# One attention-and-MLP kernel on one core: a reordered start, dummy matmuls, and heads 0 and 1 taken in turn

## The chip, the cores and the metric

The kernel runs on one core of one Trainium2 chip. The metric is the device time of one execution in microseconds (us). Two kinds of number appear below. The *time* of an execution is the metric; the *span* is what the profile of one execution covers, from its first to its last recorded instruction, and is 1.7 to 2.1 us shorter. TensorE is called PE, its weight loads PEld, VectorE DVE, ScalarE ACT, GpSimd POOL, SyncE SP. The *granted clock* is the profile's record of the share of full speed at which PE was allowed to run. A *bank* is a tile of PSUM, the memory that matmuls write to: transposes, Q and the output projection take theirs in turn from a ring of three (`mi_tile`), so a new one waits until the engine that reads the old one is done (in e6 below, 0.46 us from one Q matmul to the next for this reason, against 0.21 in e8).

## The reference

One transformer block with adaptive layer norm, 2048 rows of width 448, 16 heads of 256, an MLP of width 1792. Cut to what matters:

```python
mod = silu(c) @ w_mod                      # six vectors of 448: sa, ca, ga, sb, cb, gb
h = layernorm(x) * (1 + ca) + sa
q = h @ wq                                 # per head: 2048 x 256
p = softmax(q @ k_cache.T / 16)            # per head: 2048 x 2048
x = x + ga * ((p @ v_cache) @ wo)          # summed over 16 heads
h = layernorm(x) * (1 + cb) + sb
x = x + gb * ((gelu(h @ w_gate) * (h @ w_up)) @ w_down)
```

## The kernel before

The rows are cut into four row blocks of 512. A *unit* is one head times one row block: sixteen steps `j`, each with two score matmuls (`st`), one exp on ACT (`E`), two output matmuls (`oT`) and one addition of `E` to the row sums on DVE (`esum`). All other work of the attention (norms, Q projections, loads) hangs at chosen steps as `fill(u, j, f)`: `f` is emitted after step `j` of unit `u`. Engines execute in the order of emission, so a fill that waits blocks its engine (a Q fill at 50 us left PE idle for 0.43 and 0.28 us, with score matmuls emitted behind it).

The **prelude** is all that comes before the first scores: load x and w_mod, layer norm of row block 0, modulation columns, transposes, Q of head 0.

```python
    c_row load on ACT;  load_x(nc.sync, 0);  load_wm(0, WA)
    wq[0] = load_wq(0)
    kTs[0] = load_k(0, parts=2)          # DMA transposes, two halves
    load_x(nc.sync, 2); load_wm(WA, 3 * D); wos[0] = load_wo(0); load_x(nc.sync, 3)
    wq[1] = load_wq(1)
    ...                                  # (cut) silu of c
    load_x(nc.scalar, 1)
    vs[0] = load_v(0, nc.scalar)
    ...
    ln = LN(("a", 0), x_bf[0], ca1p_c, sa_c, mi_tile)
    for t in range(4):
        if t == 1:
            silu_c()
            modc = mod_cols(0)           # 32 one-column matmuls on w_mod
        ln.stats(t)
        if t % 2 == 1:
            ln.rstd(t - 1, 2)            # POOL
    mod_cols_out(modc, sa_c, ca1p_c)     # DVE
    for t in range(4):
        ln.norm(t)                       # DVE
    ln.twin(nc.vector)                   # last 64 columns once more, for rows 64..127
    for pr in range(2):
        ln.transpose(pr)                 # PE, evicted with the modulation by DVE and ACT in turn
    q_proj(0, 0)
```

The order of units, and the fills that feed row blocks 1 to 3:

```python
    units = [(h, r) for h in range(H) for r in range(NC)]
    ...
    pn = dict(on_pool=True)              # norm on POOL
    add_ln(("a", 1), x_bf[1], ca1p_c, sa_c, at(0, 0, 1, 2, 3), at(0, 3, 3, 3, 3), at(0, 10, 11), **pn)
    fill(0, 13, lambda: q_proj(0, 1))    # row block 1: transposes on PE
    add_ln(("a", 2), x_bf[2], ca1p_c, sa_c, at(0, 6, 7, 8, 9), at(0, 9, 9, 9, 9),
           (0, 14), at(1, 8, 9, 10, 11), **pn)
    fill(1, 13, lambda: q_proj(0, 2))    # row blocks 2 and 3: turned by DMA
    ...                                  # (cut) row block 3 likewise in units 1 and 2
            if r % 2:
                fill(u, 15, lambda u=u, h=h, r=r: (emit_exp(16 * u + 17), q_pair(h + 1, r - 1)))
```

"Turned by DMA" means: the normed block `xn` is written to DRAM (`xscr`), read back by four DMA transposes (`hT<-xscr`), and modulated in place on DVE (`modulate`).

The softmax here doesn't subtract the row's maximum and nothing guards it: scores larger than these inputs give would overflow.

## Time and profile before

| | before |
|---|---|
| time, median of 4 runs | 1245.64 us |
| span of the profiled execution | 1245.2 us |
| first score matmuls that run without a stall | 16.31 us |
| stalls of PE from there to 85 us | 5.0 us in ten places |
| first gate matmul of the MLP | 1106.82 us |

From the page of the kernel before (busy time by engine, then busy tenths in 40 slices, then the chain of waits; lines in between are left out, here and in the fences below):

```profile
span 1245.2 us, 17254 instructions
PE 1229.6 (99%) x5900; PEld 550.7 (44%) x5900; DVE 797.2 (64%) x1682; ACT 715.9 (57%) x1217; POOL 77.5 (6%) x93
PE   7999999999999999999999999999999999999998
PE 93%; DVE 2%; SPq 1%; DMA 1%; issue 1%; POOL 0%; ACT 0%; DVEq 0%
```

PE is the engine to watch, but 99% does not mean that 1% is left. In this trace the record of a 512-column matmul is 379 ns long, while such matmuls start 215.6 ns apart: records overlap, and their sum says little about how much time is left. So I read PE by the distance between starts: anything over 0.2156 us per 512 columns, the distance kept through the middle of the attention, I count as a stall, even where no idle time is shown.

The timeline of PE in the prelude of the kernel before (start, length, engine, line, operation, names, shape, count, then idle time before it and what ended it):

```profile
6.78 0.24 PE L190 MATMUL modc<-scT,wm 128*128 128x1 bf16 x3 [4.42 <-DMA wm<-in_w_mod_dram]
7.48 0.93 PE L190 MATMUL modc<-scT,wm 128*128 128x1 bf16 x29 [0.45 <-DMA wm<-in_w_mod_dram]
9.41 2.49 PE L278 MATMUL tp<-id_bf,xn 128*128 128x128 bf16 x16 [1.00 <-DVE xn L247]
11.69 0.63 PE L304 MATMUL qps<-hT,wq_t 128*128 128x512 bf16 x1
12.49 3.15 PE L304 MATMUL qps<-hT,wq_t 128*128 128x512 bf16 x7 [0.17 <-ACT hT L291]
15.43 0.63 PE L345 MATMUL st<-qT,kT 128*128 128x512 bf16 x1
16.31 1.24 PE L345 MATMUL st<-qT,kT 128*128 128x512 bf16 x5 [0.25 <-ACT qT L311]
```

The Q matmuls of the prelude stand about 0.43 us apart, twice the 0.2156 us: half clock. From 16.31 us on, five score matmuls start 0.2156 us apart. The trace's clock record fits: it begins at 16.09 us, with full clock (for the time before it has no entry).

What PE waited for in the kernel before, 16 to 90 us (total us, times, longest):

```profile
PE oT L538 <- ACT E L495: 1.3, 3, 0.8
PE qps L304 <- DVE hT L266: 0.7, 2, 0.4
PE st L345 <- ACT qT L311: 0.6, 2, 0.4
PE st L345 <- DVE qT L309: 0.4, 1, 0.4
PE tp L278 <- POOL xn L242: 0.3, 1, 0.3
```

These are the idle times that the view shows, 3.3 us in nine places, of which one (0.25 us) is the start at 16.31 itself. By the distance between starts the other eight and two more cost 5.0 us. Each says that a row block was needed soon after it was ready: Q waits for the modulated block, scores wait for Q, outputs wait for an exp that stood behind an eviction on ACT.

### The profile page before, as it was taken

The numbers are of one execution on the slowest core, as the hardware profiler recorded it, in microseconds if no ns is written. First come the engines' busy times: TensorE is split into PE (matmuls) and PEld (weight loads), VectorE is DVE, ScalarE is ACT, GpSimd is POOL, SyncE is SP. The second block draws the span as 40 slices with busy tenths as digits, with TensorE's granted clock in tenths as the row PEclk, the third lists the DMA queues.
The fourth block names the chain that finished last, engine by engine and source line by source line (L and its number), as shares of the span: only waits on it lengthen the run. The fifth ranks groups of instructions, "written<-read, shape, count | busy, mean of one in ns | idle before, by whom it ended". The sixth has DMA issues, their size and how long they took to land.

```text
span 1245.2 us, 17254 instructions
## 1 busy us (share of the span) xinstructions
PE 1229.6 (99%) x5900; PEld 550.7 (44%) x5900; DVE 797.2 (64%) x1682; ACT 715.9 (57%) x1217; POOL 77.5 (6%) x93
## 2 busy tenths in 40 slices
PE   7999999999999999999999999999999999999998
PEld 3444444444444444444444444444444444444443
DVE  6766666666666666676666666666666666776543
ACT  4556666666666666666666666666666666652222
POOL 4300000000000010020202010000000000000000
PEclk9999999999999999999999999999999999999999
DMA  7354032232423041402222221404041220030110
GB/s 189 85 135 97 18 64 55 47 115 51 119 40 93 28 95 43 101 18 52 63 47 67 51 67 37 82 13 97 18 83 35 48 54 18 18 85 16 49 49 16
DMA packets 181866, 76.48 MB, mean 61 GB/s; under 512 B 150161, under 2 KB 172242, under 8 KB 181778
## 3 DMA queue, kind: packets, MB, share of 16 engines
q1 hardware_dynamic: 180720, 73.87, 25.0%
q10 hardware_dynamic: 1058, 1.51, 0.5%
q8 instruction: 46, 0.75, 0.3%
q14 instruction: 42, 0.34, 0.1%
HBM read 33.67 MB, written 13.37 MB: 38 GB/s over the span
## 4 chain that ended last, share of the span: by engine, by line
PE 93%; DVE 2%; SPq 1%; DMA 1%; issue 1%; POOL 0%; ACT 0%; DVEq 0%
PE oT L538 34%; PE st L345 34%; PE wps L354 7%; PE qps L332 6%; PE dps L592 3%; PE g_ps L579 3%; PE u_ps L579 3%; PE qps L326 1%; PE g_ps L572 1%; DVE esum L535 1%; SPq L120 1%; DMA esT<-scr 0%; DMA scr<-esum 0%; DMA wq_t<-in_A_wq_dram 0%; PE qps L304 0%
## 5 line engine op out<-in xcount | busy, mean ns | idle before, releaser
L495 ACT ACTIVATE E<-st 128x512 bf16<-128x512 f32 x1024 | 608.3, 598 | 311.7 <-PE st L345 307.7
L538 PE MATMUL oT<-E,v_h 128*128 128x512 bf16 x2048 | 609.0, 379 | 1.9 <-ACT E L495 1.7
L345 PE MATMUL st<-qT,kT 128*128 128x512 bf16 x2048 | 609.5, 379 | 1.1 <-ACT qT L311 0.6
L535 DVE TENSOR_TENSOR esum<-esum,E 128x512 bf16<-128x512 bf16 x896 | 397.0, 443 | 163.4 <-ACT E L495 136.3
L538 PEld LDWEIGHTS <-v_h 128*128 128x128 bf16 x2048 | 199.6, 98 | 246.0 <-DVE oTn L501 10.6
L345 PEld LDWEIGHTS <-kT 128*128 128x128 bf16 x2048 | 200.3, 98 | 229.1 <-issue 1.9
L359 DVE SCALAR_TENSOR_TENSOR x_acc<-wps,inv,x_acc 128x448 f32<-128x448 f32 x240 | 163.7, 682 | 145.0 <-PE wps L354 145.0
L354 PE MATMUL wps<-wo_t,oTn 128*128 128x448 bf16 x512 | 138.6, 352 | 0.2 <-DVE x_acc L359 0.2
L140 POOL TENSOR_TENSOR wo_t<-wo_t,ga_bf 128x448 bf16<-128x448 bf16 x32 | 34.8, 1107 | 912.8 <-DMA wo_t<-in_A_wo_dram 781.0
L584 ACT ACTIVATE gl<-g_ps 128x512 bf16<-128x512 f32 x56 | 33.5, 598 | 89.5 <-PE g_ps L579 89.4
L332 PE MATMUL qps<-hT,wq_t 128*128 128x512 bf16 x360 | 82.9, 380 | 0.0
L354 PEld LDWEIGHTS <-oTn 128*128 128x128 bf16 x512 | 50.1, 98 | 60.7 <-issue 0.5
L337 DVE CAST qT<-qps 128x512 bf16<-128x512 f32 x60 | 41.5, 691 | 35.9 <-PE qps L332 35.6
L502 ACT CAST oTn<-oT 128x512 bf16<-128x512 f32 x64 | 37.6, 587 | 45.0 <-PE oT L538 45.0
L339 ACT CAST qT<-qps 128x512 bf16<-128x512 f32 x60 | 35.2, 587 | 46.8 <-PE qps L332 46.8
L585 DVE TENSOR_TENSOR hhT<-gl,u_ps 128x512 bf16<-128x512 bf16 x56 | 38.4, 687 | 36.1 <-PE u_ps L579 36.1
L332 PEld LDWEIGHTS <-wq_t 128*128 128x128 bf16 x360 | 32.8, 98 | 48.1 <-issue 12.7
L579 PEld LDWEIGHTS <-wgu 128*128 128x128 bf16 x336 | 30.6, 98 | 44.8 <-issue 11.9
L514 DVE TENSOR_REDUCE inv<-esT 128x4 f32<-128x512 bf16 x64 | 43.5, 679 | 4.5 <-DMA esT<-scr 4.5
L579 PE MATMUL g_ps<-hT,wgu 128*128 128x512 bf16 x168 | 45.7, 381 | 0.0
L579 PE MATMUL u_ps<-hT,wgu 128*128 128x512 bf16 x168 | 45.4, 379 | 0.0
L501 DVE CAST oTn<-oT 128x512 bf16<-128x512 f32 x64 | 44.2, 690 | 0.9 <-PE oT L538 0.9
(71 smaller groups left out, 317.1 us busy)
## 6 DMA issues: line engine op xcount, KB each, us to landing
scr<-esum SPq DMA_DIRECT2D x64, 128.0 KB, 2.0
wo_t<-in_A_wo_dram SPq DMA_DIRECT2D x16, 224.0 KB, 6.3
wq_t<-in_A_wq_dram SPq DMA_DIRECT2D x16, 192.0 KB, 5.0
xscr<-xn SPq DMA_DIRECT2D x6, 512.0 KB, 2.9
out_dram<-ob SPq DMA_DIRECT2D x16, 112.0 KB, 1.7
wd<-in_B_w_down_dram SPq DMA_DIRECT2D x2, 784.0 KB, 4.8
x_all<-in_A_x_dram SPq DMA_DIRECT2D x3, 448.0 KB, 4.1
wgu<-in_B_w_gate_dram SPq DMA_DIRECT2D x1, 1344.0 KB
```

The lines of the kernel that those rows point to most:

```text
L332: nc.tensor.matmul(qps[:], lhsT=wq[h][:, ch, dc * P:(dc + 1) * P], rhs=hT[("a", r)][:, ch, :], start=False, stop=(ch == 2),)
L337: nc.vector.tensor_copy(out=qTs[(h, r)][:, dc, :], in_=qps[:])
L345: nc.tensor.matmul(st[:], lhsT=kTs[h][:, dc, j * P:(j + 1) * P], rhs=qTs[(h, r)][:, dc, :], start=(dc == 0), stop=(dc == 1),)
L354: nc.tensor.matmul(wps[:], lhsT=oTn[:, dc, t * P:(t + 1) * P], rhs=wos[h][:, dc, :], start=(dc == 0), stop=(dc == 1),)
L359: nc.vector.scalar_tensor_tensor(out=x_acc[r][:, t, :], in0=wps[:], scalar=inv[:, t:t + 1], in1=prev[:, t, :], op0=ALU.mult, op1=ALU.add,)
L495: nc.scalar.activation(out=E[:], in_=sts.pop(g)[:], func=ACTF.Exp, scale=inv_sqrt_dh)
L501: nc.vector.tensor_copy(out=oTn[:, 0, :], in_=oT[0][:])
L514: nc.vector.tensor_reduce(out=inv[:], in_=esT[:], axis=mybir.AxisListType.X, op=ALU.add)
L535: nc.vector.tensor_tensor(out=esum[:], in0=esum[:], in1=E[:], op=ALU.add)
L538: nc.tensor.matmul(oT[i][:], lhsT=vs[h][:, j, i * P:(i + 1) * P], rhs=E[:], start=(j == 0), stop=(j == NKS - 1),)
L579: nc.tensor.matmul(ps[fc, i][:], lhsT=wgu[:, 3 * i + ch, fc * P:(fc + 1) * P], rhs=hr[:, ch, :], start=False, stop=(ch == 2),)
L585: nc.vector.tensor_tensor(out=hhT[:, fc, :], in0=gl[:], in1=ps[fc, 1][:], op=ALU.mult)
```

## The change

Its intent is to start the attention earlier and to feed its first units without stalls. Its core, with cuts:

```diff
-    kTs[0] = load_k(0, parts=2)
-    load_x(nc.sync, 2) ... load_x(nc.sync, 3)
+    vs[0] = kv.tile([P, NKS, Dh], BF16, name="v_h")
+    kTs[0] = load_k(0, parts=2, between=lambda i: v_part(vs[0], 0, 8 * i, 8 * i + 8, nc.sync))
     wq[1] = load_wq(1)
+    kTs[1] = load_k(1)
+    vs[1] = load_v(1)
...
-            in_=x2d[r * 512:(r + 1) * 512, :].rearrange("(t p) d -> p t d", p=P)
+        v = x2d[r * 512:(r + 1) * 512, :].rearrange("(p t) d -> p t d", p=P)   # out likewise
...
+    def warm_pe(n):                      # dummy matmuls, result unused
+        for _ in range(n):
+            nc.tensor.matmul(wpt[:], lhsT=id_bf[:], rhs=wz[:], start=True, stop=True)
+    warm_pe(10)
     load_x(nc.scalar, 1)
-    vs[0] = load_v(0, nc.scalar)
...
-    mod_cols_out(modc, sa_c, ca1p_c)
     for t in range(4):
+        if t == 2:
+            mod_cols_out(modc, sa_c, ca1p_c)
         ln.norm(t)
-    ln.twin(nc.vector)
-    for pr in range(2):
-        ln.transpose(pr)
-    q_proj(0, 0)
+        nc.scalar.copy(...)              # the twin of tile t
+        ...                              # four transposes of tile t
+        if t % 2:
+            warm_pe(1)
+    for ch in (0, 2, 1, 3):
+        ln.put(ch, tps[ch // 2][:, ch % 2, :], ch // 2)   # chunks 0,1 on DVE, 2,3 on ACT
+    q_one(0, 0)                          # chunk 3 as two half-height matmuls side by side
-    units = [(h, r) for h in range(H) for r in range(NC)]
+    units = [(h, r) for r in range(NC) for h in range(2)]
+    units += [(h, r) for h in range(2, H) for r in range(NC)]
...
+    fill(0, 12, lambda: q_one(1, 0))
+    fill(0, 0, load_rest)                # rest of w_mod, wo of head 0, x block 2
...
+    add_ln(("a", 1), x_bf[1], ca1p_c, sa_c, at(0, 1, 2, 3, 4), at(0, 6, 7, 8, 9), (0, 9),
+           at(1, 1, 2, 3, 4))            # norm on DVE, turned by DMA
+    ...                                  # blocks 2 and 3 likewise, two units later each
+    for r in range(1, NC):
+        fill(2 * r - 1, 11, lambda r=r: q_two(((0, r), (1, r))))
...
+            if (u, j) in fills:
+                emit_exp(g + 2)          # exp ahead of every fill
```

From head 2 on the units run as before.

More of the change, by code (lines that the diff above doesn't have):

```diff
@@ L102, in load_wq @@
         wq_t = wts.tile([P, DCH, Dh], BF16, name="wq_t")
-        if h == 0:
-            nc.gpsimd.memset(wq_t[DL:P, 3, :], 0.0)
         nc.sync.dma_start(
@@ L108, in load_wq @@
         )
-        for i in range(1 if h == 0 else 2):
+        for i in range(2):
             nc.sync.dma_start(
@@ L113, in load_wq, with load_k @@
         return wq_t
-    def load_k(h, parts=1):
+    def load_k(h, parts=1, between=None):
         kT = kv.tile([P, 2, SK], BF16, name="kT")
@@ L123, in load_k, with v_part, load_v @@
                 )
-        return kT
-    def load_v(h, eng=nc.sync):
+            if between is not None:
+                between(i)
+        return kT
+    def v_part(v_h, h, a, b, eng):
+        eng.dma_start(
+            out=v_h[:, a:b, :],
+            in_=A_v_cache[0, h, a * P:b * P, :].rearrange("(s p) d -> p s d", p=P),
+        )
+    def load_v(h):
         v_h = kv.tile([P, NKS, Dh], BF16, name="v_h")
-        eng.dma_start(out=v_h[:], in_=A_v_cache[0, h].rearrange("(s p) d -> p s d", p=P))
+        v_part(v_h, h, 0, NKS, nc.sync)
         return v_h
@@ L140, in scale_wo, with load_x @@
             nc.gpsimd.tensor_tensor(out=wo_t[:, cc, :], in0=wo_t[:, cc, :], in1=ga_bf[:], op=ALU.mult)
-    def load_x(eng, r):
-        eng.dma_start(
-            out=x_bf[r], in_=x2d[r * 512:(r + 1) * 512, :].rearrange("(t p) d -> p t d", p=P)
-        )
+    def load_x(eng, r, t0=0, n=4):
+        v = x2d[r * 512:(r + 1) * 512, :].rearrange("(p t) d -> p t d", p=P)
+        eng.dma_start(out=x_bf[r][:, t0:t0 + n, :], in_=v[:, t0:t0 + n, :])
     def load_wm(a, b):
@@ L157 @@
     wq[0] = load_wq(0)
-    kTs[0] = load_k(0, parts=2)
-    load_x(nc.sync, 2)
-    load_wm(WA, 3 * D)
-    wos[0] = load_wo(0)
-    load_x(nc.sync, 3)
+    vs[0] = kv.tile([P, NKS, Dh], BF16, name="v_h")
+    kTs[0] = load_k(0, parts=2, between=lambda i: v_part(vs[0], 0, 8 * i, 8 * i + 8, nc.sync))
     wq[1] = load_wq(1)
+    kTs[1] = load_k(1)
+    vs[1] = load_v(1)
     cps = mi_tile([P, DCH], F32, "cps")
@@ L170 @@
         )
+    wz = consts.tile([P, 512], BF16, name="wz")
+    nc.vector.memset(wz[:], 0.0)
+    wpt = aps.tile([P, 512], F32, tag="st", bufs=3, name="wpt")
+    def warm_pe(n):
+        for _ in range(n):
+            nc.tensor.matmul(wpt[:], lhsT=id_bf[:], rhs=wz[:], start=True, stop=True)
+    warm_pe(10)
     sg = consts.tile([P, DCH], F32, name="sg")
@@ L269, in modulate, with put @@
             )
+        def put(self, ch, a, on_act):
+            o = hT[self.key][:, ch, :]
+            if on_act:
+                nc.scalar.activation(
+                    out=o, in_=a, func=ACTF.Identity,
+                    scale=self.c1p[:, ch:ch + 1], bias=self.s[:, ch:ch + 1],
+                )
+            else:
+                nc.vector.tensor_scalar(
+                    out=o, in0=a, scalar1=self.c1p[:, ch:ch + 1], scalar2=self.s[:, ch:ch + 1],
+                    op0=ALU.mult, op1=ALU.add,
+                )
         def transpose(self, pair):
@@ L282, in transpose @@
             for i in range(2):
-                ch = pair * 2 + i
-                o, a = hT[self.key][:, ch, :], tp[:, i, :]
-                if i == 0:
-                    nc.vector.tensor_scalar(
-                        out=o, in0=a, scalar1=self.c1p[:, ch:ch + 1], scalar2=self.s[:, ch:ch + 1],
-                        op0=ALU.mult, op1=ALU.add,
-                    )
-                else:
-                    nc.scalar.activation(
-                        out=o, in_=a, func=ACTF.Identity,
-                        scale=self.c1p[:, ch:ch + 1], bias=self.s[:, ch:ch + 1],
-                    )
@@ L296 @@
-    qTs = {}
-    def q_proj(h, r):
-        qT = qpool.tile([P, 2, 512], BF16, name="qT")
-        hr = hT[("a", r)]
-        for dc in range(2):
-            qps = mi_tile([P, 512], F32, "qps")
-            for ch in range(DCH):
-                nc.tensor.matmul(
-                    qps[:], lhsT=wq[h][:, ch, dc * P:(dc + 1) * P], rhs=hr[:, ch, :],
-                    start=(ch == 0), stop=(ch == DCH - 1),
-                )
-            if dc == 0:
-                nc.vector.tensor_copy(out=qT[:, dc, :], in_=qps[:])
-            else:
-                nc.scalar.copy(out=qT[:, dc, :], in_=qps[:])
-        qTs[(h, r)] = qT
@@ L314, in q_pair, with q_out, q_rest @@
-    def q_pair(h, r0):
+                self.put(pair * 2 + i, tp[:, i, :], i)
+    qTs = {}
+    def q_out(h, r, dc, qps):
+        if dc == 0:
+            nc.vector.tensor_copy(out=qTs[(h, r)][:, dc, :], in_=qps[:])
+        else:
+            nc.scalar.copy(out=qTs[(h, r)][:, dc, :], in_=qps[:])
+    def q_rest(h, r, dc, qps, start, stop):
+        half = slice(dc * DL, (dc + 1) * DL)
+        nc.tensor.matmul(
+            qps[:], lhsT=wq[h][half, 3, dc * P:(dc + 1) * P], rhs=hT[("a", r)][half, 3, :],
+            start=start, stop=stop,
+        )
@@ new lines, in q_full, with q_one @@
+    def q_full(h, r, dc, ch, qps, start, stop):
+        nc.tensor.matmul(
+            qps[:], lhsT=wq[h][:, ch, dc * P:(dc + 1) * P], rhs=hT[("a", r)][:, ch, :],
+            start=start, stop=stop,
+        )
+    def q_one(h, r):
+        qTs[(h, r)] = qpool.tile([P, 2, 512], BF16, name="qT")
+        qps = [mi_tile([P, 512], F32, "qps") for _ in range(2)]
+        for i, ch in enumerate((0, 2, 1)):
+            for dc in range(2):
+                q_full(h, r, dc, ch, qps[dc], i == 0, False)
+        for dc in range(2):
+            q_rest(h, r, dc, qps[dc], False, True)
+        for dc in range(2):
+            q_out(h, r, dc, qps[dc])
@@ L315, in q_pair, with q_two @@
+    def q_two(hrs):
         outs = []
-        for r in (r0, r0 + 1):
+        for h, r in hrs:
             qTs[(h, r)] = qpool.tile([P, 2, 512], BF16, name="qT")
@@ L322, in q_pair @@
                     qps = aps.tile([P, 512], F32, tag="st", bufs=3, name="qps")
-                outs.append((r, dc, qps))
-        for r, dc, qps in outs:
-            half = slice(dc * DL, (dc + 1) * DL)
-            nc.tensor.matmul(
-                qps[:], lhsT=wq[h][half, 3, dc * P:(dc + 1) * P], rhs=hT[("a", r)][half, 3, :],
-                start=True, stop=False,
-            )
-        for r, dc, qps in outs:
-            for ch in range(3):
-                nc.tensor.matmul(
-                    qps[:], lhsT=wq[h][:, ch, dc * P:(dc + 1) * P], rhs=hT[("a", r)][:, ch, :],
-                    start=False, stop=(ch == 2),
-                )
-            if dc == 0:
-                nc.vector.tensor_copy(out=qTs[(h, r)][:, dc, :], in_=qps[:])
-            else:
-                nc.scalar.copy(out=qTs[(h, r)][:, dc, :], in_=qps[:])
+                outs.append((h, r, dc, qps))
+        for h, r, dc, qps in outs:
+            q_rest(h, r, dc, qps, True, False)
+        for h, r, dc, qps in outs:
+            for ch in range(3):
+                q_full(h, r, dc, ch, qps, False, ch == 2)
+            q_out(h, r, dc, qps)
     def st_mms(u, j):
@@ L365 @@
     for t in range(4):
+        ln.stats(t)
         if t == 1:
+            ln.rstd(0, 2)
             silu_c()
             modc = mod_cols(0)
-        ln.stats(t)
-        if t % 2 == 1:
-            ln.rstd(t - 1, 2)
-    mod_cols_out(modc, sa_c, ca1p_c)
+    ln.rstd(2, 2)
+    hT[("a", 0)] = hpool.tile([P, DCH, 512], BF16, name="hT")
+    tps = [mi_tile([P, 2, 512], BF16, "tp") for _ in range(2)]
     for t in range(4):
+        if t == 2:
+            mod_cols_out(modc, sa_c, ca1p_c)
         ln.norm(t)
-    ln.twin(nc.vector)
-    for pr in range(2):
-        ln.transpose(pr)
-    q_proj(0, 0)
-    units = [(h, r) for h in range(H) for r in range(NC)]
+        nc.scalar.copy(out=ln.xn[:, t, D:DCH * P], in_=ln.xn[:, t, 3 * P:D])
+        for ch in range(DCH):
+            nc.tensor.transpose(
+                out=tps[ch // 2][:, ch % 2, t * P:(t + 1) * P],
+                in_=ln.xn[:, t, ch * P:(ch + 1) * P], identity=id_bf[:],
+            )
+        if t % 2:
[5 more added lines that the diff above has]
+    units += [(h, r) for h in range(2, H) for r in range(NC)]
     fills = {}
@@ L388, in rep, with load_rest @@
             nc.vector.tensor_copy(out=scT_rep[:, k, :], in_=scT[:, k:k + 1].to_broadcast((P, P)))
-    fill(0, 15, rep)
-    fill(1, 0, lambda: mod_rep(2, ga_bf))
-    fill(1, 1, lambda: scale_wo(wos[0]))
+    def load_rest():
+        load_wm(WA, 3 * D)
+        wos[0] = load_wo(0)
+        load_x(nc.sync, 2)
+    fill(0, 12, lambda: q_one(1, 0))
+    fill(0, 0, load_rest)
+    fill(1, 1, rep)
+    fill(1, 3, lambda: mod_rep(2, ga_bf))
+    fill(1, 4, lambda: scale_wo(wos[0]))
+    fill(1, 14, lambda: wos.update({1: load_wo(1)}))
+    fill(2, 1, lambda: scale_wo(wos[1]))
+    fill(2, 0, lambda: load_x(nc.sync, 3))
     fill(3, 0, lambda: load_wm(3 * D, 6 * D))
@@ L422, in at @@
         return [(u, j) for j in js]
-    pn = dict(on_pool=True)
-    add_ln(("a", 1), x_bf[1], ca1p_c, sa_c, at(0, 0, 1, 2, 3), at(0, 3, 3, 3, 3), at(0, 10, 11), **pn)
-    fill(0, 13, lambda: q_proj(0, 1))
-    add_ln(("a", 2), x_bf[2], ca1p_c, sa_c, at(0, 6, 7, 8, 9), at(0, 9, 9, 9, 9),
-           (0, 14), at(1, 8, 9, 10, 11), **pn)
-    fill(1, 13, lambda: q_proj(0, 2))
-    add_ln(("a", 3), x_bf[3], ca1p_c, sa_c, at(1, 2, 3, 4, 5), at(1, 5, 5, 5, 5),
-           (1, 10), at(2, 6, 7, 8, 9), **pn)
@@ L432 @@
-    fill(2, 13, lambda: q_proj(0, 3))
-    for u, (h, r) in enumerate(units):
-        if h + 1 < H:
-            if r == 0:
-                def ld(h=h):
-                    kTs[h + 1] = load_k(h + 1)
-                def ld2(h=h):
-                    vs[h + 1] = load_v(h + 1)
-                    wos[h + 1] = load_wo(h + 1)
-                    if h + 2 < H:
-                        wq[h + 2] = load_wq(h + 2)
-                fill(u + 2 * (h == 0), 0, ld)
-                fill(u + 1 + (h == 0), 8 * (h == 0), ld2)
-            if r == 3:
-                fill(u, 0, lambda h=h: scale_wo(wos[h + 1]))
-            if r % 2:
-                fill(u, 15, lambda u=u, h=h, r=r: (emit_exp(16 * u + 17), q_pair(h + 1, r - 1)))
+    add_ln(("a", 1), x_bf[1], ca1p_c, sa_c, at(0, 1, 2, 3, 4), at(0, 6, 7, 8, 9), (0, 9),
+           at(1, 1, 2, 3, 4))
@@ new lines, with load_h, k, v @@
+    add_ln(("a", 2), x_bf[2], ca1p_c, sa_c, at(2, 1, 2, 3, 4), at(2, 6, 7, 8, 9), (2, 10),
+           at(3, 3, 4, 5, 6))
+    add_ln(("a", 3), x_bf[3], ca1p_c, sa_c, at(3, 13, 14, 15, 15), at(4, 2, 3, 4, 5), (4, 5),
+           at(5, 3, 4, 5, 6))
+    for r in range(1, NC):
+        fill(2 * r - 1, 11, lambda r=r: q_two(((0, r), (1, r))))
+    def load_h(h, us, ts):
+        def k():
+            kTs[h] = load_k(h)
+        def v():
+            vs[h] = load_v(h)
+            wos[h] = load_wo(h)
+        def w():
+            wq[h] = load_wq(h)
+        def q(r):
+            q_two(((h, r), (h, r + 1)))
+        fill(us[0], ts[0], k)
+        fill(us[1], ts[1], v)
+        fill(us[2], ts[2], w)
+        fill(us[3], ts[3], lambda: scale_wo(wos[h]))
+        fill(us[4], 15, lambda: q(0))
+        fill(us[5], 15, lambda: q(2))
@@ L450 @@
+    load_h(2, (7, 7, 4, 8, 6, 7), (0, 4, 8, 2))
+    for h in range(3, H):
+        u = 4 * h - 4
+        load_h(h, (u, u + 1, max(u - 3, 6), u + 3, u + 1, u + 3), (0, 0, 0, 0))
+    for u, (h, r) in enumerate(units):
         if h == H - 1 and r in (2, 3):
@@ L547 @@
                 ph, pr, po, psums = pend[:4]
-                if j == 7:
+                wj = (12, 13, 14, 15) if u == 1 else (9, 11, 13, 15)
+                if j == (10 if u == 1 else 7):
                     pinv = psums()
-                if j in (9, 11, 13, 15):
-                    wo_tile(ph, pr, (j - 9) // 2, po, pinv)
+                if j in wj:
+                    wo_tile(ph, pr, wj.index(j), po, pinv)
         pend = (h, r, oTn, sums)
@@ L599, in down @@
             f()
-        row = r * 512 + t * P
-        nc.sync.dma_start(out=out2d[row:row + P, :], in_=ob[:])
+        rows = out2d[r * 512:(r + 1) * 512, :].rearrange("(p t) d -> p t d", p=P)
+        nc.sync.dma_start(out=rows[:, t, :], in_=ob[:])
     mfill = {}
```

## The prediction

> **What bounds the kernel.** TensorE. The page shows PE busy 99% of a 1245.2 us span and 93% of the chain of waits; in the timeline 512-column matmuls follow each other every 0.2156 us through the attention, so its middle gets no faster unless matmuls go. What can be won lies in the first 85 us. From matmul spacing in the timeline: (a) the prelude: the first unstalled score matmuls start at 16.3 us; (b) ten stalls between 26 and 77 us of 0.24 to 1.0 us, 5.0 us in sum (waits for E, qT, the Pool-made xn, and late modulated hT).
>
> **The change, costed.**
> - Prelude. x in contiguous rows; norm and transposes tile by tile; the four evictions of hT (DVE 0.54, ACT 0.78 us each), now alternating, run two by two from two banks; dummy matmuls while PE waits 4.5 us for w_mod. Now: w_mod landed 7.4, norm 8.96 to 10.27, transposes to 11.9, hT complete 13.3, Q projection 11.7 to 15.6 with eight matmuls about 0.43 us apart (half clock), qT at 16.3. After, my chain: statistics end 7.7, second rstd 8.85, last norm 9.6, evictions 9.9 to 11.7, last Q matmuls 12.0, qT out 12.9, scores about 13.0. Gain 3.3 us (estimate). [...] 0.43 us spacing up to 15.4, 0.2156 from 16.3. Ten dummies at 0.43 us are 4.3 us[...]; if PE stays cold the gain is about 1.5 us less.
> - Loads. V of head 0 moves from the ACT queue, where it landed at 13.8 and slowed K (second transpose landed 15.1), to pieces behind each half of K. I expect the first half of K at 10 to 11 us: not binding. K and V of head 1 are now needed at about 26 us instead of 72. Early copies moved about 350 KB per us and transposes 280, so they should land at 20 to 23: enough.
> - Q projections of heads 0 and 1: 60 full passes become 56 (half-height pairs run together); one saved in the prelude, three after it: 3 x 0.2156 = 0.65 us.
> - Row block 1 is turned by DMA instead of PE: 16 transposes, 0.9 us of PE.
> - Stalls: norm leaves Pool (3.3 us per block) for DVE, units of heads 0 and 1 alternate so each row block has twice the time, exp is issued before fills, Q projections sit mid-unit. I expect 3.5 of the 5.0 us back, less 0.2 us for one more switch between full and half height.
>
> Nearly all of it is on the critical path, since PE is that path. After head 2 nothing changes, nor in the MLP and tail.
>
> **Prediction.** 3.3 + 0.65 + 0.9 + 3.3 = about 8 us: 1237.5 us, 8 in 10 between 1233.5 and 1241.5. Faster by over 2% 0.01 (that needs 25 us, more than prelude and stalls hold), within 2% 0.98, slower 0.01.
>
> **What would show it.** Timeline: first unstalled scores near 13; prelude Q matmuls 0.22 us apart; no PE wait over 0.5 us from there to 85 us; none for kT or v_h of head 1. The first gate matmuls of the MLP (1106 now) should be earlier by the same 8 us as the end.
>
> **What would make it wrong.** Clock still half in the prelude; K and V of head 1 late; DVE blocked in order by modulation waiting for the DMA turn, which queues behind loads on SP, so that E buffers run out; new stalls around mid-unit projections.

The sum comes to 3.3 + 0.65 + 0.9 + 3.3 = 8.15 us. The 3.3 us of the prelude assume full clock there, and that dummy matmuls would bring it was the author's assumption: the trace of the kernel before shows only that the Q matmuls ran at half clock (0.43 us apart up to 15.4 us) and the scores at full clock (0.2156 from 16.3). The 1.5 us for a PE that stays cold (at half clock) are an estimate from that trace: seven Q passes at 0.43 instead of 0.2156 us. The same trace has the other rates: the DMA engines moved 354 KB per us from 2.6 to 6.0 us, and 263 from 8.5 to 13.8, where K was being transposed and V copied; four half-height Q matmuls took 0.54 us from 54.77 on, that is two passes of 0.2156 and 0.1 us more, and the two full matmuls just before them 0.53, 0.1 more as well: the 0.2 us of the switch. That V slowed K was a reading of it: the second transpose of K took 9.7 us from issue to landing beside V, and 5.1 in the kernel after, with V issued behind it.

## The result, and the profile after

The change is worth 5.7 us by the medians: 1240.1 us (1239.74 to 1243.15, 9 runs) against 1245.78 us (1244.68 to 1247.2, 13 runs). The ratio is 0.9957 (95% interval 0.9948 to 0.9967). Ratios are the mean time of one kernel's fast runs over that of the other's of the same rounds, so not quite the ratio of these medians; 0.43% of 1245.8 us is 5.4 us, and the interval is 4.1 to 6.5 us: the 8 us of the forecast lie outside it.

From the page of the kernel after:

```profile
span 1238.9 us, 17256 instructions
PE 1229.0 (99%) x5896; PEld 550.2 (44%) x5896; DVE 798.4 (64%) x1699; ACT 715.3 (58%) x1218; POOL 64.7 (5%) x71
PE   8999999999999999999999999999999999999998
```

The page hardly shows a difference; only the first slice of PE went from 7 to 8. The timeline of PE in the prelude of the kernel after does:

```profile
2.31 3.68 PE L181 MATMUL wpt<-wz,id_bf 128*128 128x512 bf16 x10
7.40 0.23 PE L202 MATMUL modc<-scT,wm 128*128 128x1 bf16 x3 [1.41 <-DMA wm<-in_w_mod_dram]
8.44 0.93 PE L202 MATMUL modc<-scT,wm 128*128 128x1 bf16 x29 [0.81 <-DMA wm<-in_w_mod_dram]
9.23 1.01 PE L398 MATMUL tp<-id_bf,xn 128*128 128x128 bf16 x8
10.04 0.63 PE L181 MATMUL wpt<-wz,id_bf 128*128 128x512 bf16 x1
10.46 1.06 PE L398 MATMUL tp<-id_bf,xn 128*128 128x128 bf16 x8
11.32 0.63 PE L181 MATMUL wpt<-wz,id_bf 128*128 128x512 bf16 x1
11.95 1.71 PE L326 MATMUL qps<-hT,wq_t 128*128 128x512 bf16 x6
13.59 0.39 PE L320 MATMUL qps<-hT,wq_t 64*128 64x512 bf16 x2
14.76 1.46 PE L363 MATMUL st<-qT,kT 128*128 128x512 bf16 x6 [0.78 <-DVE qT L314]
```

First scores come at 14.76 us, 1.55 us earlier than before and 1.8 us later than predicted. The second part of w_mod arrives just before 8.44 us (the trace has the landing at 8.39; it was 7.43 before). With the dummies the full clock was granted from 5.07 us on (16.09 in the kernel before), and then it fell again. The windows of the kernel after (busy us and counts of PE, PEld, DVE, ACT, POOL; then granted clock, DMA share, GB/s):

```profile
5.10:8.40 3.30, 1.11 (x7) 0.34 (x5) 3.04 (x11) 0.24 (x1) 1.38 (x4) 1.00 1.09 299
8.50:11.80 3.30, 3.30 (x47) 2.69 (x48) 1.60 (x7) 0.90 (x4) 0.46 (x1) 0.50 0.95 185
12.00:17.00 5.00, 4.14 (x19) 1.66 (x19) 1.53 (x4) 3.17 (x6) 0.00 (x0) 1.00 1.08 270
```

The clock records are full from 5.07, half from 8.48, full from 11.90: steps of 3.413 us. In the step 5.07 to 8.48 PE had little to do (1.11 us of matmul records in 3.30), since it waited for w_mod, and the next step was granted half clock, just while the sixteen transposes ran. Whether the one follows from the other is taken up under e3.

What PE waited for in the kernel after, 16 to 90 us:

```profile
PE wps L372 <- DVE qT L314: 0.6, 1, 0.6
PE oT L585 <- ACT oTn L549: 0.2, 1, 0.2
```

By distance between starts three stalls remain, 0.39 at 31 us, 0.76 at 46 us, 0.24 at 86 us: 1.4 us instead of 5.0.

The budget of the two profiled executions:

| stretch | before | after | gain | predicted |
|---|---|---|---|---|
| start to first unstalled scores | 16.31 | 14.76 | 1.55 | 3.3 |
| first scores to first gate matmul | 1090.51 | 1085.70 | 4.81 | 4.85 (0.65 + 0.9 + 3.3) |
| first gate matmul to end | 138.39 | 138.47 | -0.1 | 0 |
| span | 1245.2 | 1238.9 | 6.3 | about 8 |

So in this pair of profiles the attention part came out as forecast, and the missing time is in the prelude. The split at the first gate matmul is less firm than the table looks: the two repeats of the kernel before (b2, b3 below) have 1089.92 and 1089.79 us in the second row and 139.00 and 139.09 in the third, the repeat of the change (a2) has 1085.61 and 138.58. Against these bases the second row gains 4.1 to 4.3 us and the third 0.4 to 0.6; only their sum, 4.7 us, is the same each time.

About 0.3 us more is lost outside the spans: time minus span was 1.7 to 1.9 us in three profiled executions before, and 2.0 to 2.1 in two after. The record lists both for every timed run: all runs of the change, e1 and e3 have 2.0 to 2.1, all of e2, e4 and e6 to e10 have 1.7 to 1.8. No view shows what that is.

### The profile page after: what moved, and what is told of

It is laid out like the page before. It is cut to its first block, busy times and chain, and to the rows that moved or that the text cites. A ratio compares the mean times of both kernels' runs of the same rounds, so it can differ in the third digit from the quotient of the medians.

```text
span 1238.9 us, 17256 instructions
## 1 busy us (share of the span) xinstructions
PE 1229.0 (99%) x5896; PEld 550.2 (44%) x5896; DVE 798.4 (64%) x1699; ACT 715.3 (58%) x1218; POOL 64.7 (5%) x71
## 4 chain that ended last, share of the span: by engine, by line
PE 93%; DVE 2%; SPq 2%; DMA 1%; issue 1%; POOL 0%; ACT 0%; DVEq 0%
PE oT L585 34%; PE st L363 34%; PE wps L372 8%; PE qps L326 7%; PE dps L642 3%; PE g_ps L629 3%; PE u_ps L629 3%; PE qps L320 1%; SPq L118 1%; PE g_ps L622 1%; DVE esum L582 1%; DMA xscr<-xn 1%; DVE bst L236 0%; DMA hT<-xscr 0%; DMA esT<-scr 0%
## 5 line engine op out<-in xcount | busy, mean ns | idle before, releaser
L326 PE MATMUL qps<-hT,wq_t 128*128 128x512 bf16 x384 | 88.7, 380 | 0.1
L314 DVE CAST qT<-qps 128x512 bf16<-128x512 f32 x64 | 44.1, 691 | 40.4 <-PE qps L326 36.4
L326 PEld LDWEIGHTS <-wq_t 128*128 128x128 bf16 x384 | 35.0, 98 | 51.7 <-issue 13.1
```

The costliest lines, as they stand in the source:

```text
L314: nc.vector.tensor_copy(out=qTs[(h, r)][:, dc, :], in_=qps[:])
L326: nc.tensor.matmul(qps[:], lhsT=wq[h][:, ch, dc * P:(dc + 1) * P], rhs=hT[("a", r)][:, ch, :], start=start, stop=stop,)
```

## The experiments

Theory A: the prelude is short of the forecast because of the chain in it: w_mod lands late, transposes run at half clock, and the Q matmuls are not hidden. Rival B: the dummies bought nothing or stand in the way. Rival C: the first profile of before was an unlucky one, so the forecast started from a wrong base. Two more questions came up on the way: whether the late w_mod belongs to the changed loads, and (theory D) whether something behind the prelude takes an earlier start back.

Kernels of one call ran on the same chip, and the calls on four different chips, so times of different calls are best compared by their ratios to the kernel before. All results were correct. The single runs b2, b3 and a2: their granted clocks were 1.0, 1.0 and 0.998. "Remainder" below is first unstalled scores to the end of the span; with it each profile splits into prelude and the rest.

| run | w_mod landed | first scores | remainder | span | time, median (lowest to highest), n |
|---|---|---|---|---|---|
| before, first profile | 7.43 | 16.31 | 1228.9 | 1245.2 | 1245.78 (1244.68 to 1247.2), 13 |
| b2_before_again | 7.81 | 15.96 | 1228.9 | 1244.9 | 1246.6, 1 |
| b3_before_again | 7.49 | 16.37 | 1228.9 | 1245.3 | 1246.96, 1 |
| after, first profile | 8.39 | 14.76 | 1224.2 | 1238.9 | 1240.1 (1239.74 to 1243.15), 9 |
| a2_after_again | 7.16 | 14.07 | 1224.2 | 1238.3 | 1240.33, 1 |
| e1_no_dummies | 8.36 | 15.67 | 1223.8 | 1239.5 | 1241.92 (1240.0 to 1242.67), 4 |
| e2_x1_later | 6.96 | 14.23 | 1224.1 | 1238.3 | 1239.89 (1239.46 to 1240.46), 4 |
| e3_old_rows | 7.12 | 13.64 | 1224.2 | 1237.8 | 1240.25 (1239.88 to 1240.56), 4 |
| e4_old_prelude | 7.44 | 15.68 | 1223.5 | 1239.2 | 1241.01 (1240.57 to 1241.59), 4 |
| e6_later_and_more | 7.29 | 13.43 | 1225.1 | 1238.5 | 1240.83 (1239.78 to 1241.43), 4 |
| e8_free_bank | 7.06 | 13.66 | 1223.5 | 1237.1 | 1240.37 (1238.92 to 1242.83), 5 |
| e9_pe_turn | 7.83 | 13.82 | 1227.1 | 1240.9 | 1243.37 (1242.32 to 1244.3), 4 |
| e10_best | 7.40 | 14.14 | 1223.9 | 1238.0 | 1242.28 (1239.78 to 1244.55), 5 |

The kernel before, run beside them, had medians of 1245.27 (with e1 to e4), 1246.45 (b2 to e6), 1245.95 (e7 to e9) and 1245.59 us (e10).

### e1_no_dummies

```diff
-    warm_pe(10)
-        if t % 2:
-            warm_pe(1)
```

> The changed kernel without its twelve dummy matmuls. Theory A (w_mod, which lands at 8.39 us instead of 7.43, sets the prelude, the clock only matters for the Q projection): TensorE is cold through the transposes and the six full Q matmuls, which then stand 0.43 us apart instead of 0.22; first unstalled scores at about 15.5 to 16.3 us instead of 14.76, so the time goes up by about 1 to 1.5 us, to about 1241.3. Theory B (the dummies bought nothing, because the clock fell back to half at 8.48 us anyway; the dummy after each second transpose is itself in the way): first scores at 14.3 to 14.8 us, time the same or 0.4 us less.

First scores at 15.67 us with w_mod landing as late as in the first profile (8.36), 0.91 us later than with dummies; ratio 0.9968 against 0.9957. The timeline of PE in this run:

```profile
9.20 2.17 PE L397 MATMUL tp<-id_bf,xn 128*128 128x128 bf16 x16
11.80 1.49 PE L325 MATMUL qps<-hT,wq_t 128*128 128x512 bf16 x3 [0.42 <-DVE hT L290]
13.51 1.06 PE L325 MATMUL qps<-hT,wq_t 128*128 128x512 bf16 x2 [0.22 <-issue]
14.50 0.39 PE L319 MATMUL qps<-hT,wq_t 64*128 64x512 bf16 x2
15.67 1.46 PE L362 MATMUL st<-qT,kT 128*128 128x512 bf16 x6 [0.78 <-DVE qT L313]
```

One Q matmul's record is missing. The Q projection runs at half clock through 14.5 us: it starts 0.15 us earlier than with the dummies and its last matmuls start 0.91 us later. In this pair of profiles rival B falls: the dummies are worth about 0.9 us, and all of it lies in the Q projection. The timed runs do not separate the two kernels: the intervals of the ratios, 0.9952 to 0.9985 and 0.9948 to 0.9967, overlap. How much the dummies buy also depends on the execution, as e3 shows.

### e2_x1_later

```diff
-    load_x(nc.scalar, 1)
+    # on SP, behind the first half of K and V of head 0
+    load_x(nc.sync, 1)
```

> The changed kernel with the second block of x issued on the SP queue behind the first half of K and V of head 0, so that it no longer runs beside w_mod. Theory A: w_mod then lands at or before 7.4 us (8.39 now), the modulation columns are ready a microsecond earlier, and first scores move from 14.76 to about 13.8 us; time down by about 0.9 us. Rival (w_mod lands late for another reason, such as the third wq copy or the order in the queue): w_mod stays at 8.2 us or later and the first scores at 14.5 to 14.9.

w_mod landed at 6.96, as theory A expected, but first scores came at 14.23, not 13.8, because half clock was granted from 9.14 to 12.56 us and the Q matmuls ran in it. The time is 0.2 us below the median of the change: within its spread. Whether the later x block moved w_mod could not be read from this one run, as a2 below shows.

### e3_old_rows

```diff
-        v = x2d[r * 512:(r + 1) * 512, :].rearrange("(p t) d -> p t d", p=P)
+        v = x2d[r * 512:(r + 1) * 512, :].rearrange("(t p) d -> p t d", p=P)   # out likewise
```

> The changed kernel with the rows of x and out in the old order (896-byte rows instead of 3584-byte runs). If the long runs of x are what takes the DMA engines from w_mod: w_mod lands at about 7.5 us, x of block 1 later than 9.1, first scores at about 13.9 us, time 0.8 us less than the change. If the long runs help because x of block 0 lands earlier and the shape of the packets does not matter for w_mod: w_mod stays near 8.4, x lands 0.1 us later, first scores at 14.8 to 14.9, time the same within 0.3 us.

In the profile all went as the first branch said: w_mod at 7.12, x of block 1 at 9.28, first scores at 13.64. But the median was 1240.25, no better than the change. The contiguous rows therefore gained nothing that these runs can show, and the profile alone would have suggested a loss.

The expectation did not consider the clock. In the change's second profile (a2 below) w_mod landed as early, at 7.16, and yet first scores came 0.43 us later than here. There the clock came on at 5.29 and fell to half from 8.70 to 12.11, and from the end of the last norm to the first scores took 4.36 us; here it came on at 7.48 and stayed full, and the same stretch took 3.81. Of the six profiles with ten dummies, four lost the clock again (the first profile, a2, e2, e10: 4.14 to 4.65 us for this stretch) and two kept it (e3 and e9, which got it at 7.27: 3.81 in both). Without dummies it was 5.08 (e1). Against that one profile the ten dummies bought between 0.4 and 1.3 us. How busy PE was in the first step at full clock does not tell the two kinds apart: matmul records fill 2.41 of 3.3 us in e2, which lost the clock, 2.40 in e3 and 2.19 in e9, which kept it. Nor does the wait for w_mod: 0.40 us in e2, 1.07 in e9. What decides it stays open.

### e4_old_prelude

```diff
-    for t in range(4):  ... norm, copy, four transposes, dummies tile by tile ...
-    q_one(0, 0)
+    # norms, one copy, transposes and evictions in the old order; Q one output after the other
```

> The changed kernel with the compute order of the prelude as it was (all norms after the modulation columns, one copy of the tail columns on DVE, transposes after all norms, evictions alternating bank by bank, Q one output after the other, no dummies), new loads kept. Prelude and the rest should add up: everything after the first scores keeps its 4.8 us gain (first scores to first gate matmul 1085.7 us), and the first scores come at 16.3 us or, as w_mod is now a microsecond later, at 17.0 to 17.5; time about 1242 to 1243. If the loads alone had made the prelude shorter (K no longer slowed by V), first scores would come at 15.5 or earlier.

Neither branch was met: first scores at 15.68, since w_mod landed at 7.44 this time and the full clock came at 13.69 (16.09 in the first profile of before), and the time is 1241.01, 0.9 us above the change. Set against w_mod, the start is 8.24 us after it here, 7.31 in e1 (new order, no dummies), and 6.37 and 6.91 in the two profiles of the change. So in these profiles, counted from w_mod, the new order is worth 0.9 us and the dummies another 0.4 to 0.9; with one or two profiles of each, and the clock coming at another moment in each, this is a rough size. The remainder is 1223.5 us: the gain of the attention part does not depend on the prelude; it is even a little larger when the start is late, which theory D takes up.

### b2_before_again, b3_before_again

Kernel: the one before, unchanged.

> The kernel before, unchanged, profiled once more. Its profiled execution took 1247.09 us, the second longest of 13, while their median is 1245.78. Theory C (the profile I predicted from caught a late grant of the full clock, at 16.09 us): in another execution the clock comes on at another moment, up to 3.4 us earlier, and the first unstalled scores move with it, between 14.6 and 16.3 us; span between 1243 and 1245.3 us. Rival (the spread comes from the loads): the clock comes on near 16 again, and the first scores differ by less than 0.3 us.

> The same once more: theory C expects yet another moment for the clock, and the span to follow it, at about half a microsecond of span for each microsecond of later clock between 12 and 16 us; the rival expects neither to move.

The clock came on at 14.42 and 15.71 us instead of 16.09, and first scores at 15.96 and 16.37. So the moment of the clock does vary from execution to execution: the first and the last lie 1.67 us apart. (The 3.4 us of theory C are the distance of the clock records in the change's profile; that the clock could move by that much was an assumption, and these runs do not show it.) It moved the start by only 0.4 us, but the effect is larger: in b2 w_mod landed 0.38 us later than in the first profile, which hides part of it. From the last norm to the first scores b2 took 5.32 us and the other two 6.04, so 1.67 us of clock were worth 0.7 us. Still, theory C explains little of the shortfall, since the mean start of the three is 16.2.

The remainder is 1228.9 us in all three, so the spread of these spans lies in the prelude. Inside the remainder two differences cancel: the stall at 77 us (1.01 us in the first profile) is 0.46 in b2, so that the first gate matmul comes 0.6 us earlier, counted from first scores, and b2 loses as much again in the MLP, where the first profile has no such wait:

```profile
1164.54 0.39 PE L572 MATMUL g_ps<-hT,wgu 64*128 64x512 bf16 x1 [0.44 <-DVE hT L266]
```

### a2_after_again

Kernel: the changed one, unchanged.

> The changed kernel, unchanged, profiled once more (its first profile was of a 1241.01 us execution, the median is 1240.1). If the late landing of w_mod (8.39 us) belongs to the changed loads, it lands at 8.2 to 8.5 again; if it is chance from execution to execution, as the two runs of the same loads with 8.36 and 7.44 suggest, it can land at 7.1 to 7.6, and then first scores come at 13.5 to 14.3 us instead of 14.76 and the span is about 1238.0 us.

w_mod landed at 7.16, so the 8.39 of the first profile is chance, and first scores came at 14.07. The same loads at the head of the SP queue, beside x block 1 on the ACT queue, gave 8.39, 8.36, 7.83, 7.44 and 7.16 us (after, e1, e9, e4, a2). With x block 1 later on the SP queue it was 6.96, 7.29, 7.06 and 7.40 (e2, e6, e8, e10). How x block 1 would hold w_mod up, no run shows. From these nine landings I hold it likely, not shown, that moving x block 1 saves about 0.6 us (the means are 7.84 and 7.18; the throttled execution of e7, also with the later x block, had 7.55).

The prelude of this execution, on which the account at the end rests:

```profile
9.01 0.70 DVE L259 TENSOR_SCALAR xn<-x_all,mv,rs 128x448 bf16<-128x448 bf16 x2 [0.22 <-POOL rs L244]
10.32 1.00 DVE L291 TENSOR_SCALAR hT<-tp,ca1p_c,sa_c 128x512 bf16<-128x512 bf16 x2 [0.61 <-PE tp L398]
10.54 1.45 ACT L286 ACTIVATE hT<-tp,sa_c,ca1p_c 128x512 bf16<-128x512 bf16 x2 [0.55 <-PE tp L398]
10.92 2.06 PE L326 MATMUL qps<-hT,wq_t 128*128 128x512 bf16 x6
12.91 0.39 PE L320 MATMUL qps<-hT,wq_t 64*128 64x512 bf16 x2
14.07 1.46 PE L363 MATMUL st<-qT,kT 128*128 128x512 bf16 x6 [0.78 <-DVE qT L314]
```

### e6_later_and_more

```diff
-    warm_pe(10)
+    warm_pe(15)          # and x block 1 later, as in e2
```

> The changed kernel with the second block of x on the SP queue behind the first half of K and V, and fifteen dummies instead of ten before w_mod, so that TensorE works until about 7 us. If the later x block is what made w_mod land at 6.96 us, it does so again, and the clock that fell back to half at 9.14 us in the run with ten dummies now stays full: first scores at 13.3 to 13.7 us instead of 14.23 there, time about 1239.3. If more dummies only hold up the modulation columns (clock late, dummies at half speed until 8 us): first scores at 14.2 or later.

The clock stayed full from 5.23 us on. First scores at 13.43 us, as expected, and yet the time was 1240.83, not 1239.3 (ratio 0.9958): the remainder had grown to 1225.1 us. Of the 1.3 us of earlier start, 0.9 were given back. The timeline of PE in e6 shows where:

```profile
41.86 0.61 PE L324 MATMUL qps<-hT,wq_t 64*128 64x512 bf16 x4 [0.37 <-DVE hT L282]
46.56 0.55 PE L376 MATMUL wps<-wo_t,oTn 128*128 128x448 bf16 x2 [0.54 <-DVE qT L318]
51.90 0.38 PE L589 MATMUL oT<-E,v_h 128*128 128x512 bf16 x1 [0.39 <-DVE oTn L552]
```

The Q projection of row block 1 waits for its hT, and then DVE, which had been held, is late with qT and oTn. By distance between starts: 0.53, 0.70 and 0.55 us. DVE in e6, as the timeline has it:

```profile
36.50 0.41 DVE L282 TENSOR_SCALAR hT<-hT,ca1p_c,sa_c 128x512 bf16<-128x512 bf16 x1 [4.40 <-DMA hT<-xscr]
41.73 3.06 DVE L586 TENSOR_TENSOR esum<-esum,E 128x512 bf16<-128x512 bf16 x6
```

DVE stands idle 4.4 us, in order, in front of a block that is still being turned by DMA, and afterwards works off a backlog of six row-sum additions. The trace has the four parts of hT landing between 36.5 and 40.4 us; the write to DRAM was issued at 27.2 behind K and V of head 1, the rest of w_mod, wo and x block 2, and the first transpose could be issued only at 33.9. In the first profile of the change the transposes are issued from 34.2 and the idle time is 3.14 us. The turn does not come earlier when the prelude ends earlier: in the seven profiles with this order behind the prelude (the change, a2, e1 to e4, e6) first scores range from 13.43 to 15.68 us, and the first transpose is issued at 33.4 to 34.4, without relation to them. The two late starters, e1 and e4, have none of the three stalls. How much is lost also depends on the turn: in e3, with first scores at 13.64 and the first transpose at 33.4, the stalls were 0.53 and 0.35 us, and the remainder, 1224.2, was that of the change.

### e7_turn_before_x2

```diff
         wos[0] = load_wo(0)
-        load_x(nc.sync, 2)
+    fill(0, 10, lambda: load_x(nc.sync, 2))     # behind the turn of row block 1; otherwise as e6
```

> The run with later x block and fifteen dummies, and besides the 448 KB load of x block 2 issued behind the DMA turn of row block 1 instead of ahead of it. Theory D (after the prelude a second wall follows: the turn of row block 1 waits in the SP queue and on the DMA engines for the loads, hT lands at 36.5 to 40.4 us whatever the prelude does, so an earlier start is given back as stalls at 41.1, 45.6 and 51.1 us, 1.8 us in sum): hT now lands about 1.3 us earlier, the stall of Q on hT at 41 us (0.53) goes and the one after it shrinks; first scores stay near 13.4, the time from first scores to the end falls from 1225.07 to about 1224.0 us. If the stalls have nothing to do with the turn: still 1225 us and the same three stalls.

Its profile can't be used: that execution took 1847.55 us at a mean granted clock of 0.654. The other four took 1239.33 to 1241.82 us. The question was answered by the next run, which contains this edit.

### e8_free_bank

```diff
-        qps = [mi_tile([P, 512], F32, "qps") for _ in range(2)]
+        qps = [mi_tile([P, 512], F32, "qps")]
+        qps.append(aps.tile([P, 512], F32, tag="oT", bufs=2, name="qps"))   # head 0 only; otherwise as e7
```

> The same as the kernel with the turn before x block 2, and besides the second accumulator of the first Q projection in a PSUM bank that nobody uses yet, instead of the bank of the first transposed tile, which must first be evicted by DVE. If that bank is what holds the second Q matmul 0.46 us after the first (10.61 to 11.07 in the run with fifteen dummies), it follows at once, 0.22 us later, Q ends about 0.3 us earlier relative to the first eviction, and first scores come at about 13.1 us. If the order of the evictions is what holds it, nothing moves.

In the profile theory D is borne out. What PE waited for in e8, 14 to 90 us, whole:

```profile
PE st L371 <- DVE qT L318: 0.8, 1, 0.8
PE oT L593 <- ACT oTn L557: 0.2, 1, 0.2
```

DVE's longest wait for the turn fell from 4.4 to 1.0 us, the stalls at 41, 46 and 52 us are gone, and the remainder is 1223.5 us, 1.6 below e6. The first transpose is issued at 30.9 instead of 33.9. Two edits differ from e6 here, but the bank belongs to the first Q projection alone, and e10, again with both, issues it at 32.1 and has no stall over 0.41 us. The timed runs do not show the 1.6 us: the ratios are 0.9961 (0.9949 to 0.9974) here and 0.9958 (0.9941 to 0.9974) in e6.

The bank shows in the same profile. The Q projection in e6 and then in e8, timeline of PE:

```profile
10.61 1.71 PE L330 MATMUL qps<-hT,wq_t 128*128 128x512 bf16 x6 [0.23 <-DVE hT L295]
12.26 0.39 PE L324 MATMUL qps<-hT,wq_t 64*128 64x512 bf16 x2
```

```profile
11.10 1.46 PE L330 MATMUL qps<-hT,wq_t 128*128 128x512 bf16 x6 [0.23 <-DVE hT L295]
12.49 0.39 PE L324 MATMUL qps<-hT,wq_t 64*128 64x512 bf16 x2
```

The six matmuls take 0.25 us less, because the second no longer waits until DVE has evicted the tile whose bank it takes (starts 0.21 instead of 0.46 us apart). But first scores came at 13.66, not 13.1: the clock came on late (6.75 us), the fifteen dummies ran mostly at half clock, and the modulation columns could start only at 7.90 although w_mod had landed at 7.06. The dummies stand before the modulation columns in PE's order, and at half clock they held them up for 0.84 us here.

### e9_pe_turn

```diff
-    add_ln(("a", 1), ..., at(0, 6, 7, 8, 9), (0, 9), at(1, 1, 2, 3, 4))
+    add_ln(("a", 1), ..., at(0, 6, 7, 8, 9), at(0, 13, 14))     # transposes on PE again
```

> The changed kernel with row block 1 turned on TensorE again (16 transposes in unit 0 at steps 13 and 14, evicted by DVE and ACT), everything else kept. The prediction put the transposes at 0.9 us of TensorE time; theory D says that in exchange the stall of 0.5 to 0.8 us behind the late hT goes. So first scores to end would go from 1224.2 to 1224.3 to 1225.0 us: 0.9 more work, up to 0.8 less stall, plus what E waits for while ACT evicts hT (0.8 in the kernel before). If the turn by DMA cost nothing, it would be 1225.0 to 1225.9.

From first scores to the first gate matmul it took 1086.66 us, 1.0 more than the 1085.70 and 1085.61 of the change: about the 0.9 us of transposes that I had costed, with stalls of 1.1 us in sum (0.53 and 0.59) where the two profiles of the change have 1.4 and 1.1. The other 1.9 us came where I expected nothing: 1.4 at the seam to the MLP and 0.6 behind the last addition on DVE, in the last store. What PE waited for in e9 between 1090 and 1110 us:

```profile
PE u_ps L621 <- DVE x_acc L377: 1.2, 1, 1.2
```

The change has no wait in that stretch. A likely cause is that two tiles more from a ring of three banks shift which bank the first `u_ps` gets, so that it lands on one that DVE has yet to read; that was not tested.

### e10_best

```diff
     # x block 1 later (e2), x block 2 behind the turn (e7), free bank (e8), ten dummies
```

> The changed kernel with its ten dummies, x block 1 behind the first half of K and V, x block 2 behind the DMA turn, and the free bank for the second Q accumulator. With fifteen dummies the runs spread from 1238.9 to 1242.8 us; if that spread comes from dummies that run at half clock and hold up the modulation columns, ten dummies keep the runs within about 1.2 us (as the run with ten dummies and the later x block did, 1239.46 to 1240.46). First scores at 13.4 to 14.0 us, first scores to end 1223.4 to 1223.6 us, time 1238.3 to 1239.5 us, so about 0.7 to 1.5 us below the change. If the spread comes from elsewhere, it will again be 2 us or more.

A miss. The profiled execution was nearly as expected inside (first scores 14.14, remainder 1223.9, no stall over 0.41 us up to 90 us), but took 1239.78 us, and the other four took 1240.34, 1244.55, 1244.34 and 1242.28 us: ratio 0.9979 (0.9965 to 0.9993), probably worse than the change (0.9948 to 0.9967; the intervals just meet). By the expectation's own test the spread does not come from fifteen cold dummies. In the two slowest the mean granted clock was 0.997, against 0.998 to 1.0 in all runs of the change; one step of 3.413 us at half clock takes 0.0014 off that mean, so by this estimate it was two such steps or so. That accounts for part of it at most, as two steps at half clock cost no more than 3.4 us even if PE were busy throughout. What makes the spread of e7, e8 and e10 (2.5, 3.9 and 4.8 us between their fast runs; 3.4 in the change itself, by one run of nine) is left open: only one execution of each left a trace, the one of e7 is throttled, and the other two do not show it. No kernel here is shown to beat the change.

## Why the prediction was right or wrong

The range held (1240.1 us in 1233.5 to 1241.5), but the gain was 5.7 us, not 8. It held because it was wide: 1240.1 is near its slow end. Point by point:

- **PE bounds it, only the first 85 us can be won:** right. The three spans of before differ by their preludes alone. But a gain in the first 85 us can be lost later: from the first gate matmul to the end the kernel before took 138.39, 139.00 and 139.09 us, longer where it came there earlier (b2, b3).
- **Attention part, 0.65 + 0.9 + 3.3 = 4.85 us:** right in sum, 4.81 us in the first pair of profiles. It is 4.1 to 4.3 against the other two profiles of before, and 4.7 by the remainders (1228.9 against 1224.2), so the close match is partly luck. Stalls fell from 5.0 to 1.4 us where I had said 1.5 (b2 had 4.4 of them before any change). Of the terms only the transposes were tried by themselves (e9: 1.0 for 0.9 us). That the alternating units, and not the mid-unit Q or the earlier exp, removed the stalls was argued, not shown.
- **Prelude, 3.3 us: this is the step that failed, by size.** "My chain" had scores at 13.0; measured 14.76 and 14.07. In the better execution, with w_mod early, the statistics and norms came as written (last norm ended 9.71, forecast 9.6). The chain then went wrong in two links. Last norm to first eviction I put at 0.3 us; it was 0.61 at half clock (0.40 in e6 at full clock). Last eviction to the end of Q I put at 0.3 us, as if only two matmuls were left; it was 1.32 us, because the six full matmuls weren't hidden. At full clock it is 0.99 (e6, e3, e9), and with a free bank as well 0.73 (e8): half clock cost 0.3 us and the bank, that of the first transposed tile, another 0.3. The remaining 0.4 is in the forecast itself: in e8 the six matmuls start as soon as the first eviction is done, one every 0.2156 us, and the last pair still starts 0.35 us after the last eviction has ended and takes 0.39. In the first profile the late w_mod cost another 0.9 us up to the last norm, since the modulation columns stand between norm 1 and norm 2 in DVE's order; first scores came 0.7 us later than in a2, as Q ran at full clock there.
- **"If PE stays cold the gain is about 1.5 us less":** in kind right, in form wrong. PE did not stay cold: it was released at 5.07 and lost the clock again at 8.48. That the wait for w_mod behind the dummies is the reason is not shown: e2 lost the clock with a wait of 0.40 us, and e9 kept it with one of 1.07. Without any dummies the start was 0.9 us later (e1).
- **First half of K "not binding":** right (11.5 us, first scores 14.8). **K and V of head 1 "at 20 to 23":** too early. They landed at 24.8 and 29.6 us in the first profile; no PE matmul waits for them (first uses at 29.4 and 32.0 us), but V was only 2.4 us ahead.
- **"DVE blocked in order by modulation waiting for the DMA turn":** named as a risk and it happened: 3.1 us of idle DVE in the change, 4.4 in e6. In the change it costs one stall, 0.76 us against the forecast of no wait over 0.5; with an earlier start it cost 1.8 us (e6) and 0.9 (e3), so this wall could have taken back part of a shorter prelude.
- **Base:** the 8 us were counted in one profile. Of three profiles of before the mean start is 16.2 us, of two after 14.4: 1.8 us. Together with the remainder's 4.7 that is 6.5 us of span, and about 6.2 of time when the 0.3 us outside the spans are taken off; the medians say 5.7 and the ratio 5.4, and 6.2 lies within the interval of 4.1 to 6.5.

## What to carry to other kernels

Cost a start-up chain link by link at the clock that will be granted there (a Q matmul took 0.43 or 0.22 us here), and ask of each "hidden" group of matmuls which PSUM bank it takes and who must first read it (0.25 us in e8). When a prelude is shortened, look for the next thing that has a fixed arrival time (here a DMA turn behind some three megabytes of loads): the earlier start turns into a wait there (e6 gave 0.9 of 1.3 us back). For gains of a microsecond take several profiles and trust the timed runs; a single trace here misplaced one landing by 1.2 us, and several better-looking traces belonged to kernels that timed no better.

## What these runs show of the clock and the loads, and leave open

- The clock records of the change's profile are 3.413 us apart (5.07, 8.48, 11.90). What decides the clock of the next step is not shown. A stretch with 1.11 us of matmul records in 3.3 was followed by half clock (after), one with 2.35 in 3.3, 32 of its 42 matmuls one column wide, also (a2), and stretches with 3.15 (e6), 2.40 (e3) and 2.19 (e9) were not. So the share of busy time alone does not decide it.
- One execution on one core (e7) ran at a mean granted clock of 0.654, with the digit 6 (six tenths) in each of the 40 slices of its page, and took 1847.55 us where its neighbours took 1239 to 1242; the records of its score matmuls are 515 ns long in the mean, against 379 in those of before, after, e8 and e10. Why is open.
- Landing times spread between executions of one program: the same w_mod load landed at 7.16 and at 8.39 us.
- So do whole executions: 4.8 us on 1240 in e10, in a program whose profiled execution shows nothing unusual.
